# Order of the up projection and place of the state scaling in a fused retention, FFN and routed-FFN kernel

## The chip, the cores and the metric

The kernel runs on one core of one Trainium2 chip. The metric is device time in microseconds (us): the median over the runs of the program. TensorE is called PE here, VectorE DVE, ScalarE ACT and GpSimd POOL, as in the profile.

## The reference, cut to what matters

```python
# 4 batches, 8 heads, 576 positions, 64 per head
ret = (q @ k.T / 8) * gamma_h ** (i - j)        # for i >= j, else 0
x = (ret @ v), heads side by side               # 2304 tokens x 512
h = x @ w_in                                    # 512 x 2048
g = h * tanh(softplus(h))
y = g @ w_out                                   # 2048 x 512
...                                             # routing: 8 experts, 288 tokens each, then relu FFN per expert
```

The change lies in the first two parts: the retention (called attention in the kernel) and the dense FFN. The routing and the expert FFN follow them and are not edited.

## The kernel before, in words

`first_part` computes attention and dense FFN together. The FFN is cut into 9 blocks of 256 tokens times 16 slices of 128 hidden units, which makes 144 **steps** (`plan`, the list `steps`). The first 48 steps mix blocks 0 to 2; from there the blocks follow one another. Each engine executes its instructions in the order in which the Python code issues them, so the loop `for i in range(len(steps) + YL)` is the schedule. In the words of this text, step i issues:

- **S(i)**, the slot work (`slots.get(i)`): for one attention chunk of 128 or 64 positions, in different steps, the scores (`a_scores`, PE L219, DVE L224, POOL L228 and L233), the output (`a_out`, PE L243 and L248, then the evacuation to `xh` on ACT L254 and to `xl` on DVE L255) and the state (`a_state`, PE L273, then the scaling into `SD`, L281 or L285). Transposes and products of the router's logits (`turned`, `products`, L382 to L394) are slot work too.
- **tanh(i)** and the two ACT instructions behind it (`ff_a1`, L327 to L329, tile `d`), then DVE's product and reciprocal (L335, L340), two products on POOL (L347, L348) or one on DVE in steps that convert (L345), and the product with h (`ff_b2`, L353, issued one step later).
- **H(i+1)**, the up projection of the next step (`ff_h`, L318): 12 products of 128x256 into one half of a PSUM tile `ph`. Steps 2m and 2m+1 share a tile; there are two tiles, `ph0` and `ph1`.
- **gh(i-2), gl(i-2)** (`ff_b3`, L359 on ACT, L360 on POOL, or on DVE in steps that convert): the high and low part of g.
- **Y(i-3)**, the down projection (`ff_y`, L412, 6 products of 128x512; in the last block `ff_y_last`, L448, 12 of 128x256). YL is 3.

H(0) is issued ahead of the loop's first step. An H for an odd step may not write its half before tanh of the even step has read the other half of the same tile.

In the steps that still convert the 64-bit weights to float32 halves (`now` or `old` is set; ACT L156, L159, L174, DVE L163, L168, POOL L177), ACT and DVE carry those instructions as well.

The state of a chunk is kept in one PSUM bank as four 128x128 squares of which only two 64x64 blocks on the diagonal are used; the other two blocks hold zeros. `a_state` copies the two blocks into `SD`, times a factor per partition: for chunks 2 to 7 with 8 ACT instructions of 64x64 (L285), for the others with 2 DVE instructions of 64x256 (L281). `a_out` of the next chunk reads `SD` as its weights (L243).

Near the end of the loop `idle` holds short pieces that are issued one or two a step, among them `Grid.pieces` (L637 to L661): DVE takes the largest and smallest logit (L638 to L640, tile `g_mm`), PE transposes them (L644), DVE reduces (L645, L646), PE spreads the result (L650).

Of the kernel before, what the change touches and what calls it, by code (L numbers as in the profile page):

```python
# [15 lines left out]
AF = mybir.ActivationFunctionType  # L16
ALU = mybir.AluOpType

P = 128
# [45 lines left out]
def plan():  # L65


    spread = lambda a, b, n: [a + (b - a) * k // (n - 1) for k in range(n)]
    own = {i: (0, f) for f, i in enumerate([0, 1, 2, 3] + spread(6, ENDS[0], NF - 4))}
    free = [i for i in range(3 * NF) if i not in own]  # L70
    lead = [i for i in free if i < BEGIN2]
    rest = [i for i in free if BEGIN2 <= i]
    near = [i for i in rest if i <= ENDS[1]]
    ones = lead + [near[k] for k in spread(1, len(near) - 1, NF - len(lead))]
    own.update({i: (1, f) for f, i in enumerate(ones)})
    own.update({i: (2, f) for f, i in enumerate(i for i in free if i not in ones)})
    steps = [own[i] for i in range(3 * NF)]
    steps += [(n, f) for n in range(3, NB) for f in range(NF)]
    return steps


def first_part(ctx, tc, att, att_ht, att_hn, dtab, qtab, ktab, stab, wi, wo, wgb, ydram, L, constants, cst, begin, grid):
    nc = tc.nc
# [12 lines left out]
    S_ = big.tile([P, 8, 4], F32, name="st")  # L96
    SD = big.tile([P, 4, P], F32, name="sd")

    steps = plan()
# [42 lines left out]
    class convert:  # L142
# [18 lines left out]
        def x(self):  # L161
            w0 = self.w0
            nc.vector.scalar_tensor_tensor(w0, self.w1, 0x80000000, w0, op0=ALU.bitwise_and,  # L163
                                           op1=ALU.bitwise_or)
# [16 lines left out]
    def x_block(n):  # L181
        if n not in xT:
            if n == 2:
                xT[n] = [sp.tile([P, KT, TB], F32R, tag="x2", name=f"x{k}2", bufs=2) for k in "hl"]
            else:
                xT[n] = [work.tile([P, KT, TB], F32R, tag="x" + k, name="x" + k, bufs=2) for k in "hl"]
        return xT[n]
# [8 lines left out]
    def bank(tag=None):  # L196
        if not tag:
            tag = att_tags[turn[0] % len(att_tags)]
            turn[0] += 1
        return psum.tile([P, 4, P], F32, tag=tag, name="b_" + tag)  # L200
# [3 lines left out]
    def since(ci):  # L204


        b, s0, n = CHUNKS[ci]
        r = CHUNKS[RESTART]
        return s0 - r[1] if ci >= RESTART and b == r[0] else s0
# [47 lines left out]
    def a_state(ci):  # L257
        b, s0, n = CHUNKS[ci]
        if s0 + n == S:
            return  # L260
        a = at_tiles[ci]
        ps_state = state[0]
        if ci == RESTART:
            att_tags.remove("B")
            ps_state = state[0] = bank("B")
            for hp in range(4):
                nc.tensor.matmul(ps_state[:, hp, :], cst["ident"], SD[:, hp, :], start=(hp == 0),
                                 stop=False, skip_group_check=True)
        for hp in range(4):
            for s in range(2):  # L270
                r = slice(s * 64, (s + 1) * 64)
                c = slice((2 * hp + s) * D, (2 * hp + s + 1) * D)
                nc.tensor.matmul(ps_state[r, hp, r], a[:n, 2, c], a[:n, 3, c],  # L273
                                 start=(s0 == 0 and hp == 0), stop=False, skip_group_check=True)
        s0 = since(ci)
        c = (s0 + n + 64) // P - 1 + 4 if (s0 + n) % P else (s0 + n) // P - 1
        for s in range(2):
            r = slice(s * 64, (s + 1) * 64)
            q = slice(s * 64, (s + 1) * 64)
            if ci < 2 or ci > 7:  # L280
                nc.vector.tensor_mul(SD[r, :, q], ps_state[r, :, q],  # L281
                                     S_[r, c, :, None].to_broadcast([64, 4, 64]))
                continue
            for hp in range(4):
                nc.scalar.activation(SD[r, hp, q], ps_state[r, hp, q], AF.Copy, scale=S_[r, c, hp:hp + 1])  # L285

    def chunks_of(n):
        return [ci for ci, (b, s0, l) in enumerate(CHUNKS) if (b * S + s0) // TB == n]
# [13 lines left out]
        return out  # L302

    rs = work.tile([P, DM], BF, tag="scr", name="rs").bitcast(F32)
    q2 = {}
    inv = {}
    hbank = [None]
# [2 lines left out]
    def ff_h(n, f, i):  # L310
        xh, xl = x_block(n)
        if i % 2 == 0:
            hbank[0] = psum.tile([P, 2, TB], F32, tag=("ph0", "ph1")[i // 2 % 2], name="ph")
        ph = hbank[0][:, i % 2, :]
        k = 0
        for kt in range(KT):
            for w, x in ((winh, xh), (winl, xh), (winh, xl)):
                nc.tensor.matmul(ph, w[f][:, kt, :], x[:, kt, :], start=(k == 0), stop=(k == 11))  # L318
                k += 1
        q2[n, f] = ph  # L320

    def ff_a1(n, f, i, alone):

        ph = q2[n, f]
        d = work.tile([P, 2, P], F32, tag="d", name="d", bufs=2)
        df = d.rearrange("p a b -> p (a b)")
        nc.scalar.activation(df, ph, AF.Tanh, scale=0.5)  # L327
        nc.scalar.activation(df, df, AF.Square, bias=half_b, scale=-0.5)  # L328
        nc.scalar.activation(df, df, AF.Copy, bias=0.5, scale=0.5)  # L329
        u = work.tile([P, 2, P], F32, tag="u", name="u", bufs=3)  # L330
        r = u[:, 0, :]
        if alone:

            r = rs[:, i % 2 * P:][:, :P]
        nc.vector.tensor_mul(r, d[:, 0, :], d[:, 1, :])  # L335
        inv[n, f] = (d, u, r, alone)

    def ff_a2(n, f):
        r = inv[n, f][2]
        nc.vector.reciprocal(r, r)  # L340

    def ff_b1(n, f, eng):
        d, u, r, alone = inv.pop((n, f))
        if alone:
            eng.tensor_mul(u, d[:, ::-1, :], r[:, None, :].to_broadcast([P, 2, P]))  # L345
        else:
            eng.tensor_mul(u[:, 1, :], d[:, 0, :], r)  # L347
            eng.tensor_mul(u[:, 0, :], d[:, 1, :], r)  # L348
        gt[n, f] = u.rearrange("p a b -> p (a b)")
# [164 lines left out]
    old, now, nxt = c2, c3, convert()  # L514
# [8 lines left out]
    for n in range(4, NB):  # L523
        ms = micro(n)
        for j, m in enumerate(ms):
            first = 5 if n == 4 else 1
            at = FOUR[j] if n == 4 else int(first + (14 - first) / len(ms) * j)
            slots.setdefault((n - 1) * NF + at, []).extend(m)

    for x in slots.get(-1, []):  # L530
        x()
    for i in range(len(steps) + YL):
        new = i < len(steps)
        if not i:
            ff_h(*steps[0], 0)
        if i == 20:
            constants()
        if i == 62:
            stage.__exit__(None, None, None)
            late = tc.tile_pool(name="late", bufs=1)  # L540
            WG = late.__enter__().tile([P, E, DM], F32, name="WG")
            nc.sync.dma_start(WG, wgb)
        if now:
            now.x()
            now.a()
        if old:
            old.l()
        if new:
            n, f = steps[i]
            for x in slots.get(i, []):  # L550
                x()
            if i and steps[i - 1] in inv:
                ff_b1(*steps[i - 1], nc.vector)
            ff_a1(n, f, i, bool(now or old))
            if i + 1 < len(steps):
                ff_h(*steps[i + 1], i + 1)
        if new:

            eng = nc.vector if now or old else nc.gpsimd
            if i > 1:  # L560
                ff_b3(*steps[i - 2], eng)
            ff_a2(n, f)
            if i:
                ff_b2(*steps[i - 1])
            if eng is not nc.vector:
                ff_b1(n, f, nc.vector if i == len(steps) - 1 else eng)
        if i == len(steps) - 1:
            ff_b2(n, f)
            ff_b3(*steps[i - 1], nc.gpsimd)
            ff_b3(n, f, nc.vector)  # L570
        if now:
            now.h()
        old, now = now, None
        if nxt and i in CONV:
            now, nxt = nxt, convert() if done[0] < len(parts) else None
            now.x1()
            now.c()
        for k in range(2 if i % 4 == 0 or TAIL <= i < POP2 else 1):
            if idle:
                idle.pop(0)()  # L580
        if late and i > TAIL + BEGIN and not idle:
            late = late.__exit__(None, None, None)
            soon.extend(begin())
        if i >= YL:
            ff_y(*steps[i - YL], i)
# [886 lines left out]
def constants(cp, tc, ap, cst):  # L1472
    nc = tc.nc
    load_constants(cp, tc, ap, cst, (("ident", [P, P], F32), ("J", [P, NJ + 1], F32), ("SCL", [P, 3], F32),
                                     ("pri", [P, E], F32), ("tri", [P, P], BF), ("io", [P, 96], BF),
                                     ("pcv", [P, NT, 2], BF), ("WGN", [P, KT, E], F32)))
    cst["ones"] = cp.tile([P, P], BF, name="c_ones")
    nc.vector.memset(cst["ones"], 1.0)
# [69 lines left out]
```

## Time and profile before

| | |
|---|---|
| median of 3 runs | 843.76 us (842.48 to 844.92) |
| the profiled execution | 842.58 us |
| its span, first to last instruction | 840.7 us |
| mean granted PE clock | 0.97 of full speed |
| PE busy | 771.4 us (92%) |
| DVE busy | 541.6 us (64%) |
| POOL busy | 477.9 us (57%) |
| ACT busy | 441.1 us (52%) |
| first H, last Y of the loop | 18.4 us, 541.6 us |

The profile belongs to one execution; all stretches and durations are of it. The 1.9 us between its span and its time lie around the program. The loop takes 523 of the 841 us; behind it come routing and the experts.

### The profile page before, as it was taken

How to read it: one execution, taken by the hardware profiler on the slowest of the kernel's cores; microseconds unless marked ns; L12 is line 12 of the kernel's file. 1: busy time of each engine (PE TensorE's matmuls, PEld its weight loads, DVE VectorE, ACT ScalarE, POOL GpSimd, SP SyncE). 2: the span in 40 equal slices, each digit the busy share in tenths (PEclk: the TensorE clock that was granted, in tenths of full speed). 3: DMA queues.
4: the chain of work that ended last, by engine and by line, in shares of the span. 5: the costliest groups of instructions: out<-in, count | busy, mean ns of one | idle time of the engine just before them, and what ended most of it. 6: DMA issues, size and time to landing. Idle time of an engine off the chain costs nothing.

```text
span 840.7 us, 16293 instructions
## 1 busy us (share of the span) xinstructions
PE 771.4 (92%) x6151; PEld 700.1 (83%) x6151; DVE 541.6 (64%) x1271; ACT 441.1 (52%) x963; POOL 477.9 (57%) x541
## 2 busy tenths in 40 slices
PE   6688999999999999999999999939999999999993
PEld 5677777888888887888888889929989999999993
DVE  4797999555645797887988976576566653442110
ACT  2678999544544554545555554423444543554520
POOL 2543333554445576666766655314777986977811
PEclk9799999999999999999999999958999999999997
DMA  8545442001312310310110000044565664655411
GB/s 315 190 136 202 152 159 101 27 1 51 101 51 101 107 44 2 101 51 27 51 51 26 1 27 2 8 164 143 168 183 180 190 195 155 187 163 170 125 30 32
DMA packets 27321, 87.63 MB, mean 104 GB/s; under 512 B 4449, under 2 KB 5601, under 8 KB 27105
## 3 DMA queue, kind: packets, MB, share of 16 engines
q1 hardware_dynamic: 24160, 77.06, 28.2%
q0 software_dynamic: 3072, 9.44, 3.5%
q8 instruction: 50, 0.82, 0.4%
q14 instruction: 39, 0.31, 0.1%
HBM read 77.05 MB, written 9.44 MB: 103 GB/s over the span
## 4 chain that ended last, share of the span: by engine, by line
PE 64%; DVE 18%; issue 7%; ACT 5%; POOL 2%; DMA 2%; SPq 0%; DVEq 0%; POOLq 0%; ACTq 0%
PE ph L318 18%; PE hp L1263 9%; PE op L1277 8%; PE b_F L412 6%; PE b_E L412 6%; DVE u L340 2%; DVE rs L340 2%; PE cnt L978 2%; DVE raw L163 2%; DVE y L168 1%; DVE u L353 1%; PE b_D L248 1%; DVE u L335 1%; PE b_A L219 1%; PE b_E L448 1%
## 5 line engine op out<-in xcount | busy, mean ns | idle before, releaser
L318 PE MATMUL ph<-xh,winh 128*128 128x256 f32 x576 | 170.5, 296 | 29.0 <-ACT d L327 21.4
L318 PE MATMUL ph<-xl,winh 128*128 128x256 f32 x576 | 161.6, 281 | 1.6 <-DVE xl L255 1.6
L318 PE MATMUL ph<-xh,winl 128*128 128x256 f32 x576 | 161.3, 280 | 0.0
L817 POOL TENSOR_TENSOR wxl<-wraw,wxh 128x1024 fp32r<-128x1024 f32 x60 | 142.3, 2397 | 29.9 <-ACT wxh L815 29.5
L318 PEld LDWEIGHTS ph<-xh,winh 128*128 128x128 f32 x576 | 109.1, 189 | 49.6 <-ACT d L327 28.0
L360 POOL TENSOR_TENSOR gl<-u,gh 128x256 fp32r<-128x256 f32 x114 | 88.6, 778 | 88.0 <-ACT gh L359 87.4
L318 PEld LDWEIGHTS ph<-xh,winl 128*128 128x128 f32 x576 | 109.7, 191 | 2.0
L318 PEld LDWEIGHTS ph<-xl,winh 128*128 128x128 f32 x576 | 109.4, 190 | 2.1 <-DVE xl L255 2.1
L340 DVE RECIPROCAL u<-u 128x128 f32<-128x128 f32 x113 | 107.7, 953 | 3.9
L327 ACT ACTIVATE d<-ph 128x256 f32<-128x256 f32 x144 | 54.5, 379 | 98.1 <-PE ph L318 84.2
L347 POOL TENSOR_TENSOR u<-d,u 128x128 f32<-128x128 f32 x112 | 52.4, 468 | 58.8 <-DVE u L340 58.7
L335 DVE TENSOR_TENSOR u<-d 128x128 f32<-128x128 f32 x113 | 48.3, 427 | 46.4 <-ACT d L329 42.8
L815 ACT ACTIVATE wxh<-wraw 128x1024 fp32r<-128x1024 f32 x64 | 67.3, 1052 | 17.1 <-DMA wraw<-in_wx_dram 17.0
L328 ACT ACTIVATE d<-d,half_b 128x256 f32<-128x256 f32 x144 | 73.5, 511 | 4.7
L348 POOL TENSOR_TENSOR u<-d,u 128x128 f32<-128x128 f32 x112 | 68.2, 609 | 8.8
L359 ACT ACTIVATE gh<-u 128x256 fp32r<-128x256 f32 x144 | 58.5, 406 | 11.3 <-DVE u L353 9.3
L329 ACT ACTIVATE d<-d 128x256 f32<-128x256 f32 x144 | 60.2, 418 | 4.5
L369 DVE SCALAR_TENSOR_TENSOR scr<-y,WG 128x512 bf16<-128x512 f32 x64 | 55.2, 862 | 0.4
L1254 DVE SCALAR_TENSOR_TENSOR htl<-hp,hth 128x288 fp32r<-128x288 f32 x64 | 28.4, 454 | 40.3 <-ACT hth L1266 39.8
L1266 ACT ACTIVATE hth<-hp 128x288 fp32r<-128x288 f32 x64 | 26.1, 408 | 52.3 <-PE hp L1263 51.8
L353 DVE SCALAR_TENSOR_TENSOR u<-u,ph 128x256 f32<-128x256 f32 x144 | 52.5, 365 | 0.3
L1263 PE MATMUL hp<-xth,wxh 128*128 128x288 f32 x256 | 50.2, 309 | 0.9 <-DVE htl L1254 0.9
(271 smaller groups left out, 1885.6 us busy)
## 6 DMA issues: line engine op xcount, KB each, us to landing
wraw<-in_wx_dram SPq DMA_DIRECT2D x64, 512.0 KB, 4.4
att<-in_att_dram SPq DMA_DIRECT2D x32, 512.0 KB, 5.0
raw<-in_wi_dram SPq DMA_DIRECT2D x16, 512.0 KB, 3.3
raw<-in_wo_dram SPq DMA_DIRECT2D x16, 512.0 KB, 3.3
ydram<-y SPq DMA_DIRECT2D x9, 512.0 KB, 2.8
WG<-in_wgb_dram SPq DMA_DIRECT2D x1, 2048.0 KB, 7.6
att<-in_att_ht_dram SPq DMA_DIRECT2D x4, 256.0 KB, 3.8
att<-in_att_hn_dram SPq DMA_DIRECT2D x4, 256.0 KB, 4.1
```

The costliest lines, as they stand in the source:

```text
L318: nc.tensor.matmul(ph, w[f][:, kt, :], x[:, kt, :], start=(k == 0), stop=(k == 11))
L328: nc.scalar.activation(df, df, AF.Square, bias=half_b, scale=-0.5)
L329: nc.scalar.activation(df, df, AF.Copy, bias=0.5, scale=0.5)
L340: nc.vector.reciprocal(r, r)
L348: eng.tensor_mul(u[:, 0, :], d[:, 1, :], r)
L353: nc.vector.scalar_tensor_tensor(g, g, -1.0, q2.pop((n, f)), op0=ALU.add, op1=ALU.mult)
L360: eng.tensor_sub(gl, g, gh.bitcast(F32))
L412: nc.tensor.matmul(py[n][t], g[:, t * P:(t + 1) * P], w[f], start=(f == 0 and w is woh and g is gh), stop=(f == NF - 1 and g is gl))
L815: nc.scalar.activation(hi, raw, AF.Copy)
L817: rest = lambda eng: eng.tensor_sub(lo, raw, hi.bitcast(F32))
L1263: nc.tensor.matmul(hp, W[kt][w][:, s], x[:, kt, :], start=(k == 0), stop=(k == 11))
L1277: nc.tensor.matmul(op, W[4 + ft // 2][w][:, s], h[:, ft, :], start=(k == 0), stop=(k == 23))
```

## The change

The state is scaled with instructions over all 128 partitions and both halves at once: one DVE instruction of 128x512 instead of two of 64x256, or four ACT instructions of 128x128 instead of eight of 64x64. The ACT instructions are no longer issued with the slot work but put into a list, `behind`, and issued behind the three ACT instructions of `ff_a1` of the same step. And H(i+1) is issued in step i only where step i converts weights; in the other steps H(i) is issued at the head of its own step, ahead of S(i).

```diff
@@ a_state
-        for s in range(2):
-            r = slice(s * 64, (s + 1) * 64)
-            q = slice(s * 64, (s + 1) * 64)
-            if ci < 2 or ci > 7:
-                nc.vector.tensor_mul(SD[r, :, q], ps_state[r, :, q],
-                                     S_[r, c, :, None].to_broadcast([64, 4, 64]))
-                continue
+        if ci < 2 or ci > 7:
+            nc.vector.tensor_mul(SD, ps_state, S_[:, c, :, None].to_broadcast([P, 4, P]))
+            return
+
+        def scale():
             for hp in range(4):
-                nc.scalar.activation(SD[r, hp, q], ps_state[r, hp, q], AF.Copy, scale=S_[r, c, hp:hp + 1])
+                nc.scalar.activation(SD[:, hp, :], ps_state[:, hp, :], AF.Copy, scale=S_[:, c, hp:hp + 1])
+
+        behind.append(scale)
@@ first_part
+    behind = []
@@ the loop
+    not_yet = lambda i: steps[i] not in q2
     for i in range(len(steps) + YL):
         new = i < len(steps)
-        if not i:
-            ff_h(*steps[0], 0)
+        if not i or new and not_yet(i):
+            ff_h(*steps[i], i)
...
             ff_a1(n, f, i, bool(now or old))
-            if i + 1 < len(steps):
+            while behind:
+                behind.pop()()
+            if now or old:
                 ff_h(*steps[i + 1], i + 1)
```

Three places show how the instructions stand.

PE, around the output of chunk 7 (step 40; `winh_89` belongs to H(40), `winh_87` to H(41), `woh_116` to Y(36), `woh_117` to Y(37)). Before:

```order
L318 MATMUL ph<-xl,winh_89 128x256
L412 MATMUL b_E<-woh_116,gh 128x512
L412 MATMUL b_E<-wol_132,gh 128x512
L412 MATMUL b_F<-woh_116,gh 128x512
L412 MATMUL b_F<-wol_132,gh 128x512
L412 MATMUL b_E<-woh_116,gl 128x512
L412 MATMUL b_F<-woh_116,gl 128x512
L243 MATMUL b_B<-att,sd 128x128 x4
L248 MATMUL b_B<-pm,att 64x128 x8
L318 MATMUL ph<-xh_602,winh_87 128x256
L318 MATMUL ph<-xh_602,winl_103 128x256
```

The same place now, where lines from L305 on have moved by one:

```order
L319 MATMUL ph<-xl,winh_89 128x256
L243 MATMUL b_B<-att,sd 128x128 x4
L248 MATMUL b_B<-pm,att 64x128 x8
L413 MATMUL b_E<-woh_117,gh 128x512
L413 MATMUL b_E<-wol_133,gh 128x512
L413 MATMUL b_F<-woh_117,gh 128x512
L413 MATMUL b_F<-wol_133,gh 128x512
L413 MATMUL b_E<-woh_117,gl 128x512
L413 MATMUL b_F<-woh_117,gl 128x512
L319 MATMUL ph<-xh_592,winh_87 128x256
L319 MATMUL ph<-xh_592,winl_103 128x256
```

Between H(40) and H(41) stood Y(36) and then S(40); now S(40) comes first and Y(37) behind it.

ACT, around the state of chunk 6 (step 9; `winh_82` and `woh_113` are converted weights). Before:

```order
L254 ACTIVATE xh_602<-b_E 128x4x128
L285 ACTIVATE sd<-b_F,st 64x64 x8
L327 ACTIVATE d<-ph 128x256
L328 ACTIVATE d<-d,half_b 128x256
L329 ACTIVATE d<-d 128x256
L359 ACTIVATE gh<-u 128x256
L174 ACTIVATE woh_113<-y_153 128x512
```

Now:

```order
L254 ACTIVATE xh_592<-b_E 128x4x128
L328 ACTIVATE d<-ph 128x256
L329 ACTIVATE d<-d,half_b 128x256
L330 ACTIVATE d<-d 128x256
L283 ACTIVATE sd<-b_F,st 128x128 x4
L360 ACTIVATE gh<-u 128x256
L174 ACTIVATE woh_113<-y_153 128x512
```

The scaling has moved behind the three instructions of tile `d`, and has half as many instructions.

PE, in step 132 of the last block, around the first transposition of `Grid` (`winh_81` belongs to H(133), `winh_80` to H(132), `woh_109` to Y(129)). Before:

```order
L318 MATMUL ph<-xh,winh_81 128x256
L318 MATMUL ph<-xh,winl_97 128x256
L318 MATMUL ph<-xl,winh_81 128x256
L644 MATMUL b_D<-c_ident,g_mm 2x128
L448 MATMUL b_E<-gh,woh_109 128x256
L448 MATMUL b_E<-gh,wol_125 128x256
```

Now:

```order
L319 MATMUL ph<-xh,winh_80 128x256
L319 MATMUL ph<-xh,winl_96 128x256
L319 MATMUL ph<-xl,winh_80 128x256
L383 MATMUL b_C<-c_ident,y 128x128 x4
L648 MATMUL b_D<-c_ident,g_mm 2x128
L449 MATMUL b_E<-gh,woh_109 128x256
```

H(133) stood between the slot work of step 132 (L382) and the transposition; now the transposition follows the slot work at once.

## Rows read from the trace of the kernel before

**Rows 1.** Stretches: busy us (xcount) of PE, PEld, DVE, ACT, POOL; PEclk, DMA share, GB/s
```profile
90.00:120.00 30.00, 27.07 (x163) 22.00 (x162) 29.16 (x64) 28.25 (x63) 10.32 (x8) 1.00 0.44 147
450.00:480.00 30.00, 29.54 (x220) 25.91 (x219) 28.17 (x57) 16.30 (x39) 20.80 (x31) 1.00 0.00 1
```

**Rows 2.** Waits of PE, 150 to 540 us: us in total, times, longest
```profile
PE ph L318 <- ACT d L327: 7.3, 8, 1.0
PE ph L318 <- DVE u L353: 2.8, 7, 0.5
PE b_A L382 <- ACT y L421: 0.5, 1, 0.5
```

**Rows 3.** Timeline of PE from 177.57 us: start, duration, instruction, idle before
```profile
177.57 1.09 PE L248 MATMUL b_B<-pm,att 128*64 128x128 f32 x16
179.63 0.39 PE L318 MATMUL ph<-xh,winh 128*128 128x256 f32 x1 [0.97 <-ACT d L327]
...
181.11 0.39 PE L412 MATMUL b_E<-woh,gh 128*128 128x512 f32 x1
...
182.48 0.28 PE L318 MATMUL ph<-xh,winh 128*128 128x256 f32 x1
```

**Rows 4.** Timeline of ACT, same stretch
```profile
178.71 0.60 ACT L254 ACTIVATE xh<-b_B 128x512 fp32r<-128x512 f32 x1 [4.49 <-PE b_B L248]
179.20 0.38 ACT L327 ACTIVATE d<-ph 128x256 f32<-128x256 f32 x1
```

**Rows 5.** Waits of DVE, 20 to 150 us
```profile
DVE rs L335 <- ACT d L329: 5.0, 4, 2.1
```

**Rows 6.** Instructions that write tile d, one row: ns min/median/max, first to last start
```profile
L335 DVE TENSOR_TENSOR rs<-d x31: 273/285/1055, 29.2 to 146.0; 128x128 f32<-128x128 f32 x31
```

**Rows 7.** Timeline of ACT, step 9
```profile
73.53 1.82 ACT L285 ACTIVATE sd<-b_F,st 64x64 f32<-64x64 f32 x8
75.37 0.39 ACT L327 ACTIVATE d<-ph 128x256 f32<-128x256 f32 x1
```

**Rows 8.** Timeline of DVE, step 9
```profile
76.78 0.29 DVE L335 TENSOR_TENSOR rs<-d 128x128 f32<-128x128 f32 x1 [2.09 <-ACT d L329]
```

**Rows 9.** Instructions that write tile sd
```profile
L285 ACT ACTIVATE sd<-b_F,st x32: 295/302/309, 32.7 to 75.0; 64x64 f32<-64x64 f32 x32
...
L281 DVE TENSOR_TENSOR sd<-b_B,st x18: 408/422/428, 214.9 to 455.9; 64x256 f32<-64x256 f32 x18
```

**Rows 10.** Instructions that write tile pm
```profile
L224 DVE TENSOR_TENSOR pm<-b_A,dt x15: 409/691/692, 6.5 to 461.2; 128x512 f32<-128x512 f32 x13, 64x256 f32<-64x256 f32 x2
```

**Rows 11.** Timeline of POOL at five places
```profile
173.26 0.73 POOL L360 TENSOR_TENSOR gl<-u,gh 128x256 fp32r<-128x256 f32 x1
...
298.19 1.29 POOL L228 TENSOR_TENSOR att<-att,qt 128x512 f32<-128x512 f32 x1
...
300.50 0.73 POOL L360 TENSOR_TENSOR gl<-u,gh 128x256 fp32r<-128x256 f32 x1
...
470.74 0.74 POOL L360 TENSOR_TENSOR gl<-u,gh 128x256 fp32r<-128x256 f32 x1 [2.83 <-ACT gh L359]
...
537.95 0.74 POOL L360 TENSOR_TENSOR gl<-u,gh 128x256 fp32r<-128x256 f32 x1 [1.13 <-ACT gh L359]
```

**Rows 12.** Timeline of PE: the first product with gl of Y(36), Y(69), Y(119)
```profile
176.12 0.39 PE L412 MATMUL b_E<-woh,gl 128*128 128x512 f32 x1
...
302.60 0.39 PE L412 MATMUL b_E<-woh,gl 128*128 128x512 f32 x1
...
473.53 0.39 PE L412 MATMUL b_E<-woh,gl 128*128 128x512 f32 x1
```

**Rows 13.** Timeline of DVE, end of the first piece of Grid
```profile
502.37 0.16 DVE L640 TENSOR_SCALAR g_mm<-g_mm 128x1 f32<-128x1 f32 x1
```

**Rows 14.** Timeline of PE: the transposition in step 132; first product with gl of Y(142)
```profile
502.74 0.27 PE L644 MATMUL b_D<-c_ident,g_mm 128*2 128x128 f32 x1
...
538.75 0.38 PE L448 MATMUL b_E<-gl,woh 128*128 128x256 f32 x1
```

## The prediction

> **What bounds the kernel now.** I read the busy time by stretch first. From 90 us, while weights are converted, DVE is busy 29.16 of 30 us and PE only 27.07; late in the loop PE is busy 29.54 of 30 and DVE 28.17, at a granted clock of 1.00 in both [rows 1]. So the loop has two parts. In the first one DVE sets the pace, with ACT close behind it; it ends at 146 us, where the tile `rs`, which only steps that convert write, is written for the 31st and last time, so these are steps 0 to 30 [rows 6]. In the second one PE sets the pace, and what can be gained there is what PE waits. The waits of PE from 150 to 540 us sum to 10.6 us in 390, in three lines: 7.3 us in 8 waits of H for tanh, 2.8 us in 7 waits of H for DVE's product with h, and one wait of 0.5 us of a transposition for the evacuated y [rows 2].
>
> One of the 8 is shown. The output of chunk 7 ends on PE at 178.66, and H(41) starts only at 179.63 [rows 3]. In between ACT evacuates that output (0.60 us) and then does tanh(40), which ends at 179.58 [rows 4]. H(41) shares its PSUM tile with H(40), so it must wait for tanh(40); tanh(40) stands behind the evacuation on ACT, and the evacuation waits for S(40). PE has nothing between S(40) and H(41). That is the place that the new order changes.
>
> **The second part: H in its own step.** Before, PE's order was H(i), Y(i-4), S(i), H(i+1). Now it is H(i), S(i), Y(i-3), H(i+1). Number and kind of PE's instructions stay the same. A Y takes 1.37 us (181.11 to 182.48) and an H 1.48 with its late second product [rows 3]. After S(40) PE now has a Y to do, 1.37 us, while tanh(40) comes 0.97 us after S(40): the wait goes, with 0.40 us to spare. The 8 waits are at most 1.0 us each [rows 2], so all of them fit under a Y: **-7.3 us**. The transposition that waited 0.5 us for the evacuated y now stands behind an H: **-0.5**. For the 2.8 us for DVE nothing changes, since H of an even step needs the same product with h as before and as much PE work lies between: 0.
>
> What pays for it is the distance between g and Y. Y(k) stood behind H(k+4), now it stands behind H(k+3): each Y comes a Y and an H earlier against the H of its own g, 1.37 + 1.38 = 2.75 us where H runs without the late product. I set the end of gl(k) and gh(k) against the product of Y(k) that needs it, for k from 32 to 127. In 15 of these 96 Ys there is less than 2.75 us, by 13.0 us in all. Three show it: Y(36), gl ends at 173.99 and its product starts at 176.12, so 2.13 us to spare and 0.6 us missing; Y(69), 301.23 and 302.60, 1.37 to spare and 1.4 missing; Y(119), 471.48 and 473.53, 2.05 and 0.7 [rows 11, 12]. But in all 15 gl or gh was late because it stands behind slot work of step k+2, on POOL (gl(69) behind the products of the scores that begin at 298.19 [rows 11]) or on ACT, and S(k+2) itself now comes a Y earlier, 1.37 us. With that the worst two come out at 0.0 and the others at +0.4 to +0.9. I take **0** here, with a bound of +13.0.
>
> Two places near the end do cost. Grid's transposition starts at 502.74, directly behind H(133), and what it needs from DVE ends at 502.53 [rows 13, 14]. H(133) no longer stands ahead of it; PE comes there 1.4 us earlier with only 0.2 us to spare: **+1.2** (bounds 0 to 1.4, since DVE's piece moves a little earlier too). And at the very end PE already waits for gl: POOL's last gl ends at 538.69 and its product in Y(142) starts at 538.75 [rows 11, 14]. What gl(142) waits for hangs on H(143), the last H, because DVE does the reciprocal of step 143 first. H(143) now has one more Y ahead of it, so this chain moves back by a Y, and nothing is left to fill the gap: **+1.4** (bounds 0.5 to 1.4; a Y of 12 products of the H's shape is taken as long as an H or a Y in [rows 3]).
>
> **The first part: the scaling behind tile d.** H is a step ahead there as before. In steps 1, 3, 7 and 9 ACT scaled the state of a chunk ahead of tanh. In step 9 the 8 instructions took 1.82 us and tanh started at 75.37, at once behind them [rows 7]; DVE had idled 2.09 us when it could begin with the result [rows 8]. These four waits are 5.0 us of a DVE that is otherwise full, the longest 2.1 [rows 5]. Now tanh comes 1.82 us earlier and the scaling stands behind d. It still stands ahead of gh and of the conversion's instructions on ACT, on which DVE waits next. A 64-column instruction takes 0.302 us [rows 9], eight together 1.82, so 0.23 each; one of 256 columns takes 0.38 [rows 4]. Four of 128 columns lie between 0.9 and 1.5 us; I take 1.1, near the 64-column row. So ACT saves 0.7 us per chunk and DVE's own chain 1.8. For steps 1 and 9, where DVE idled 2.1 each, I take 1.1 each, nearer to ACT's gain; the other two waits, 0.8 together, go. **-3.0 us** (bounds -0.6, ACT's least saving twice, and -5.0, the whole of the waits). As DVE is full to the end of this part, this shifts all that follows.
>
> The Trainium skill (ScalarE: Activation LUTs, Rules for kernel authors) budgets some 0.3 us per ACTIVATE and 0.83 ns per element. By it 8 instructions of 64 columns would take 2.8 us and 4 of 128 1.6, a saving of 1.2 us instead of 0.7, an estimate; the sum would be 1.0 us lower with it. The row of one instruction, 0.302 us, is nearly that figure, but eight in 1.82 us overlap, so here the rows decide.
>
> On DVE one instruction of 128x512 takes the place of two of 64x256: 0.69 for 2 x 0.42 us [rows 9, 10]. It saves 0.15 us of DVE per chunk; the products that read `SD` come steps later. I cost it at 0; if DVE's lag were the bound there, nine times 0.15, 1.4 us, would be gained.
>
> **Sum.** -7.3 - 0.5 + 1.2 + 1.4 - 3.0 = -8.2 us. Against the profiled execution, 842.58, that is 834.4; against the median, 843.76, which is 1.2 higher, 835.6. I forecast **835.0 us**, between the two.
>
> **The rivals.** Slower: *Y waits for g*. If the slot work does not bring gl and gh forward (because POOL or ACT reach it no earlier, or because S itself, directly behind H, then waits for DVE to free a bank), all 13.0 us come as new waits of PE before L413: 842.6 - 8.2 + 13.0 = 847.4. It decides from 8.2 of 13.0 on, that is when more than six tenths of the shortage stays. For it: the two worst places have nothing to spare even with the credit. Against it: POOL begins on the scores' operand only when the scores are done, so it does come earlier.
>
> *Given back in part*: a third of the 13.0 stays, 4.3 us: 838.7, or 839.9 from the median. For it: in stretches where DVE is busy 28.17 of 30 us [rows 1] a late row of DVE makes gh and gl late too, and no slot work moves to make up for that.
>
> *No change*: the second part's gain is handed over to DVE, so that the 7.3 us come back as waits for DVE's product, the 2.8 us growing to some 10; what is left is -3.0 + 2.6 - 0.5, so 842. Against it: where DVE is fullest, PE leaves at most 0.5 of 30 us [rows 1], so the 8 waits lie elsewhere, where DVE has more room.
>
> *More*: the first part gives its whole 5.0 us and the two places at the end cost their least, 0.5 together: 842.58 - 7.3 - 0.5 - 5.0 + 0.5 = 830.3.
>
> **How the numbers follow.** Chances: the forecast (832 to 838.5) 0.62; more than that 0.08; given back in part 0.12; no change 0.08; slower 0.10. A measurement of this kernel can tell about 0.3%, 2.5 us, from no change, so faster means below 841.3. The first three cases are faster: 0.82. The fourth is the same, 0.07 of its 0.08; the 0.01 left of it goes to slower, which is 0.11 with the last. The range has the first three cases: 830.3 to 841.0, some 0.8.
>
> **What would show it.** In the profile after: no waits of H for tanh of 1 us between 150 and 360 us; PE's timeline there with L243, L248, then L413, then L319 without a gap. In the first part no DVE wait of 2 us for d in steps 1 and 9, the tile `rs` written for the last time some 3 us earlier, at 143 us. A new wait of about 1.2 us before the transposition L648, and 1.5 us before the product with gl of Y(142). L283's four instructions together near 1.1 us. The forecast is wrong if PE's waits have new lines for L413 with gl or gh as releaser (slower or given back), if its waits for DVE's product grow, or if the last `rs` is not earlier.

## The result, and the profile after

The changed kernel takes 833.46 us (median of 4 runs, 830.91 to 836.3), the kernel before 843.12 in the runs beside it (4 runs, 840.72 to 844.92): a ratio of 0.9888, 95% interval 0.9846 to 0.993. The forecast was 835.0 (830.3 to 841.0). The profiled execution took 832.66 us, span 830.9, granted clock 0.97. The total is as forecast; two terms of the sum behind it are not, and they cancel almost.

The engines' busy time in the page after the change:

```profile
PE 770.4 (93%) x6151; PEld 704.0 (85%) x6151; DVE 537.8 (65%) x1260; ACT 434.4 (52%) x943; POOL 476.9 (57%) x541
```

PE does the same work (770.4 against 771.4 us) in a shorter span. **Second part.** Busy time by stretch, in the columns of [rows 1]; first the sums over 150 to 480 us in eleven stretches of 30, before:

```profile
sum 330.00, PE 320.38 PEld 280.23 DVE 238.81 ACT 166.92 POOL 196.47; mean PE 29.13 PEld 25.48 DVE 21.71 ACT 15.17 POOL 17.86
```

and after, with the last stretch, to be read against the last one of [rows 1]:

```profile
450.00:480.00 30.00, 30.00 (x214) 26.84 (x212) 26.80 (x55) 15.97 (x39) 20.06 (x30) 1.00 0.00 1
sum 330.00, PE 330.00 PEld 295.27 DVE 239.26 ACT 168.43 POOL 202.03; mean PE 30.00 PEld 26.84 DVE 21.75 ACT 15.31 POOL 18.37
```

PE is now busy in all of the 330 us, where 9.6 were lost. The waits of PE from 150 to 540 us, against [rows 2] (the lines L982 and L992 belong to the routing, which now begins before 540):

```profile
PE cnt L982 <- DVE ind L697: 1.2, 1, 1.2
PE b_D L648 <- DVE g_mm L644: 1.0, 1, 1.0
PE b_E L449 <- POOL gl L361: 0.5, 2, 0.3
PE b_E L449 <- ACT gh L360: 0.4, 1, 0.4
PE dg L992 <- DVE full L986: 0.3, 1, 0.3
PE cnt L982 <- ACT y L471: 0.2, 1, 0.2
```

All three lines of [rows 2] are gone, the 2.8 us for DVE among them, and no line of L413 has come. What came is the transposition's wait, 1.0 us, and 0.9 us of waits for gl and gh in the last block.

**First part.** Here nothing was gained. The waits of DVE from 20 to 150 us, against [rows 5]:

```profile
DVE raw L163 <- ACT raw L159: 3.5, 3, 1.8
DVE gl L361 <- ACT gh L360: 1.0, 1, 1.0
DVE pm L224 <- PE b_D L219: 0.4, 1, 0.4
```

The 5.0 us for `d` are gone, as forecast. But the row of `rs` that answers to [rows 6], and DVE's row of `gl`, are

```profile
L336 DVE TENSOR_TENSOR rs<-d x31: 276/285/1380, 28.9 to 147.0; 128x128 f32<-128x128 f32 x31
...
L361 DVE TENSOR_TENSOR gl<-u,gh x30: 412/420/1518, 41.2 to 530.4; 128x256 fp32r<-128x256 f32 x30
```

The last `rs` is at 147.0, not at 143 and not even at 146.0; and a product for `gl` that has a median of 0.42 us took up to 1.52. Before, its longest took 0.43. DVE works longer on about as many instructions (busy time by stretch, 30 to 90 us, before, then after; the third column is DVE's):

```profile
30.00:60.00 30.00, 24.44 (x250) 21.65 (x250) 26.56 (x49) 22.66 (x59) 13.10 (x10) 0.91 0.38 116
60.00:90.00 30.00, 25.92 (x198) 22.23 (x197) 25.43 (x52) 26.44 (x66) 11.50 (x9) 0.94 0.60 209
```

```profile
30.00:60.00 30.00, 24.45 (x250) 21.19 (x249) 28.31 (x46) 21.35 (x50) 12.53 (x9) 0.93 0.35 112
60.00:90.00 30.00, 24.39 (x190) 19.79 (x189) 28.23 (x53) 24.28 (x56) 11.65 (x9) 1.00 0.62 201
```

From the first `rs` to the last DVE issues 217 instructions in both kernels. Its idle time there fell from 6.6 to 2.0 us (new waits among them, 1.0 us of `gl` for gh), but the durations of the 217 sum to 127.7 us instead of 121.6. The largest part of these 6.1 us is that of `gl` (DVE's products from 20 us to the last `rs`: count, sum of us and mean ns, before, then after):

```profile
L360 DVE TENSOR_TENSOR gl<-u,gh 128x256 fp32r<-128x256 f32 x28 | 11.7, 418 | 0.0
...
L361 DVE TENSOR_TENSOR gl<-u,gh 128x256 fp32r<-128x256 f32 x28 | 15.0, 536 | 1.0 <-ACT gh L360 1.0
```

What lies beside a long one, in step 5 (timeline of DVE, then of POOL, after the change):

```profile
56.55 0.28 DVE L336 TENSOR_TENSOR rs<-d 128x128 f32<-128x128 f32 x1
56.75 1.50 DVE L361 TENSOR_TENSOR gl<-u,gh 128x256 fp32r<-128x256 f32 x1
58.18 0.94 DVE L341 RECIPROCAL rs<-rs 128x128 f32<-128x128 f32 x1
...
56.62 1.36 POOL L177 TENSOR_TENSOR wol<-y,woh 128x512 fp32r<-128x512 f32 x1 [2.66 <-ACT woh L174]
```

POOL's subtraction of the conversion began 0.13 us ahead of the product and ended at 57.98; the product ended at 58.25. In the same step of the kernel before, the product began 0.11 us ahead of the subtraction and kept its 0.41 us; the subtraction took 1.46 us, where its median is 1.29:

```profile
56.53 0.41 DVE L360 TENSOR_TENSOR gl<-u,gh 128x256 fp32r<-128x256 f32 x1
56.87 0.93 DVE L340 RECIPROCAL rs<-rs 128x128 f32<-128x128 f32 x1
...
56.64 1.46 POOL L177 TENSOR_TENSOR wol<-y,woh 128x512 fp32r<-128x512 f32 x1 [2.11 <-ACT woh L174]
```

### The profile page after: what moved, and what is told of

It is laid out like the page before. It is cut to its first block, busy times and chain, and to the rows that moved or that the text cites. A ratio compares the mean times of both kernels' runs of the same rounds, so it can differ in the third digit from the quotient of the medians.

```text
span 830.9 us, 16266 instructions
## 1 busy us (share of the span) xinstructions
PE 770.4 (93%) x6151; PEld 704.0 (85%) x6151; DVE 537.8 (65%) x1260; ACT 434.4 (52%) x943; POOL 476.9 (57%) x541
## 4 chain that ended last, share of the span: by engine, by line
PE 72%; DVE 13%; issue 7%; ACT 3%; POOL 2%; DMA 2%; SPq 0%; DVEq 0%; POOLq 0%; ACTq 0%
PE ph L319 20%; PE hp L1267 9%; PE b_E L413 8%; PE op L1281 8%; PE b_F L413 8%; DVE rs L341 2%; DVE raw L163 2%; PE cnt L982 2%; DVE y L168 2%; PE b_A L219 2%; PE b_D L248 1%; DVE u L346 1%; DVE hot L878 1%; PE b_E L449 1%; PE b_F L449 1%
## 5 line engine op out<-in xcount | busy, mean ns | idle before, releaser
L319 PE MATMUL ph<-xh,winh 128*128 128x256 f32 x576 | 165.1, 287 | 19.1 <-ACT d L328 12.0
L361 POOL TENSOR_TENSOR gl<-u,gh 128x256 fp32r<-128x256 f32 x114 | 85.7, 752 | 95.5 <-ACT gh L360 94.7
L336 DVE TENSOR_TENSOR u<-d 128x128 f32<-128x128 f32 x113 | 40.3, 357 | 69.7 <-ACT d L330 68.0
```

Source lines behind the costliest of these rows:

```text
L361: eng.tensor_sub(gl, g, gh.bitcast(F32))
```

## The experiments

**Theory.** All of the gain comes from the order of H. In the first part the waits for `d` did go, but DVE's instructions that take two operands from SBUF are held while POOL's subtraction L177 runs, and with an earlier tanh they meet it. **Rivals.** The scaling has a part in the second part's gain; or the scaling behind `d` delays gh and the conversion on ACT, so that DVE waits there.

All runs but 3 and 4 in one table. "Last rs" is the end of the range in the row of `rs`; "loop" is the last start of the product `b_F<-gl,woh` less that; "behind" is the span less that start. All three are of the profiled execution; times and ratios are of all runs. The kernel before was run again beside each group, with a median of 843.95 us beside runs 1 and 2, 841.98 beside 5 to 8 and 843.49 beside 9 to 12, so across groups the ratios compare, not the times.

| kernel | last rs | loop | behind | median us | ratio to before (95%) |
|---|---|---|---|---|---|
| before | 146.0 | 395.3 | 299.4 | 843.12 | |
| changed | 147.0 | 385.7 | 298.2 | 833.46 | 0.9888 (0.9846 to 0.993) |
| 1 scaling alone | 146.8 | 394.9 | 300.2 | 843.65 | 1.0002 (0.9988 to 1.0017) |
| 2 order of H alone | 146.4 | 385.6 | 300.5 | 833.89 | 0.9877 (0.9853 to 0.9902) |
| 5 reciprocal first | 156.8 | 385.2 | 298.7 | 842.63 | 1.0002 (0.9989 to 1.0016) |
| 6 subtraction in halves | 148.5 | 385.0 | 298.3 | 833.59 | 0.9899 (0.9874 to 0.9924) |
| 7 Y ahead of S | 148.2 | 414.7 | 298.1 | 862.21 | 1.0235 (1.0216 to 1.0255) |
| 8 grid behind Y | 147.1 | 384.2 | 299.1 | 831.68 | 0.9872 (0.9852 to 0.9891) |
| 9 four ahead of tanh | 146.5 | 385.6 | 300.0 | 835.23 | 0.99 (0.9879 to 0.9921) |
| 10 later L174 | 145.5 | 385.8 | 301.0 | 834.65 | 0.9889 (0.9868 to 0.991) |
| 11 old scaling, grid | 148.6 | 384.5 | 300.6 | 832.66 | 0.9868 (0.9847 to 0.9889) |
| 12 later L174, grid | 145.9 | 384.4 | 300.5 | 832.31 | 0.986 (0.9837 to 0.9882) |

The loop repeats within some tenths of a us wherever its code is the same (385.0 to 385.8 in six kernels). The part behind it, which no kernel edits, spreads over 2.9 us, so totals say nothing on 1 or 2 us.

**1. The scaling alone.** The changed scaling, every H at its old place:

```diff
-        if not i or new and not_yet(i):
-            ff_h(*steps[i], i)
+        if not i:
+            ff_h(*steps[0], 0)
...
-            if now or old:
+            if i + 1 < len(steps):
                 ff_h(*steps[i + 1], i + 1)
```

> The changed scaling (one instruction on DVE, four on ACT behind tile d) with the old place of every H. Theory (the second part's gain comes from the order of H alone, and the first part's gain is eaten by DVE instructions that get longer beside POOL's conversion subtraction): the 8 waits of PE for tanh are back, 7 to 8 us between 150 and 540 us; tile rs written for the last time at 146.5 to 147.5 us; total 842 to 845 us, no gain over the kernel before. Rival (DVE's nine shorter scalings make room for PE's waits to go): at least 3 us of the 10.6 us of waits are gone and the total is 841 or less.

Measured: ratio 1.0002, loop 394.9. The waits of PE from 150 to 540 us are back:

```profile
PE ph L319 <- ACT d L328: 7.3, 8, 1.0
PE ph L319 <- DVE u L354: 2.2, 5, 0.5
PE b_A L383 <- ACT y L422: 0.5, 1, 0.5
```

The scaling brings nothing by itself; DVE's nine shorter instructions take 0.6 us at most off the waits for DVE.

**2. The order of H alone.** The changed loop, with the old `a_state`, in place and in halves:

```diff
-        if ci < 2 or ci > 7:
-            nc.vector.tensor_mul(SD, ps_state, S_[:, c, :, None].to_broadcast([P, 4, P]))
-            return
...
+        for s in range(2):
+            r = slice(s * 64, (s + 1) * 64)
+            q = slice(s * 64, (s + 1) * 64)
...
-        behind.append(scale)
```

> The new place of H with the old scaling in place (eight instructions of 64x64 on ACT ahead of tanh, two of 64x256 on DVE). Theory: all of the gain is here; PE waits between 150 and 480 us stay under 1.5 us, tile rs is written for the last time at 145.5 to 146.5 us as before, and the total is 0 to 1.5 us below the changed kernel, 831 to 834 us. Rival (the scaling carries a part of the second part's gain, since nine chunks save 0.15 us of DVE each and four have 0.7 us of ACT less): waits of PE of 1 to 3 us remain between 150 and 480 us, and the total is 834 to 837 us.

Measured: ratio 0.9877, loop 385.6, as the changed kernel within 0.1. From 150 to 480 us no wait of H or Y is left; L648 waits 0.9. The whole gain is the order of H.

**3 and 4. Without the subtraction.** In both kernels `lo` is set to zero once, by POOL, and L177 is left out, so the low parts of the weights are missing. That changes the logits and with them the routing, and the part behind the loop grows to some 700 us; only the first part is compared.

```diff
         def l(self):
-            nc.gpsimd.tensor_sub(self.lo, self.t, self.hi.bitcast(F32))
+            pass
```

> The kernel before without POOL's subtraction in the conversion (L177): the low parts of the weights are left out (set to zero once), so POOL has none of these instructions of 1.28 us. Theory (DVE instructions with two operands in SBUF get longer while that subtraction runs): DVE's product for gl never takes over 0.6 us in steps 1 to 30, and tile rs is written for the last time 1 to 4 us earlier than 146.0 us. Rival (their length has nothing to do with POOL): single products for gl of 1.5 us stay.

> The changed kernel with the same left out as in the run before it. Theory (the 5.0 us of waits did go, and longer DVE instructions beside POOL's subtraction ate them): no product for gl over 0.6 us, and tile rs is written for the last time 2 to 5 us earlier than in the kernel before with the same left out. Rival (the scaling behind d delays gh and the conversion's instructions on ACT, so DVE waits there instead): it is written within 1 us of that kernel or later.

Measured, the rows of `rs`, before without it and changed without it:

```profile
L337 DVE TENSOR_TENSOR rs<-d x31: 275/287/898, 28.6 to 144.3; 128x128 f32<-128x128 f32 x31
```

```profile
L338 DVE TENSOR_TENSOR rs<-d x31: 271/285/1128, 27.9 to 141.7; 128x128 f32<-128x128 f32 x31
```

Without the subtraction the changed kernel is 2.6 us earlier, with it 1.0 later. Each is one execution, and with the subtraction the last `rs` of one and the same code came out up to 2.6 us apart (run 11), so the size is not sure. The sums point the same way: without it DVE's durations between the first and the last `rs` differ by 1.0 us (119.3 and 120.3) instead of 6.1, while the idle time still falls, from 8.1 to 5.2. So most of the 3.0 us of the forecast was there to be had. One product for `gl` still took 1.25 us, against the expectation; it lay beside another POOL product that reads SBUF (49.15, 1.42 us, `att<-att,kt`).

**5. The reciprocal first.** In the converting steps DVE does the reciprocal, then the product for `gl`:

```diff
+            first = eng is nc.vector
+            if first:
+                ff_a2(n, f)
             if i > 1:
                 ff_b3(*steps[i - 2], eng)
-            ff_a2(n, f)
+            if not first:
+                ff_a2(n, f)
```

> The changed kernel; in the steps that convert, DVE's reciprocal of the step is issued ahead of its product for gl (and ACT's gh behind it in program order, which leaves ACT's own order alone). Theory (the product for gl gets longer while POOL's subtraction L177 runs, the reciprocal does not): the reciprocal of 0.95 us now lies beside the subtraction of 1.28 us, no product for gl is over 0.8 us, the last write of tile rs falls to 142.5 to 145.5 us, the total to 828.5 to 831.5. Rival (a late gl holds up something else in these steps, or DVE's time was not lost there): last rs at 146 us or later, total at 832 or more.

Measured: the opposite, last `rs` at 156.8 and 842.63 us. The row of `gl` and two places (DVE, then POOL):

```profile
L361 DVE TENSOR_TENSOR gl<-u,gh x30: 360/860/967, 42.4 to 539.7; 128x256 fp32r<-128x256 f32 x30
...
103.43 0.29 DVE L336 TENSOR_TENSOR rs<-d 128x128 f32<-128x128 f32 x1
103.76 0.95 DVE L341 RECIPROCAL rs<-rs 128x128 f32<-128x128 f32 x1
104.63 0.86 DVE L361 TENSOR_TENSOR gl<-u,gh 128x256 fp32r<-128x256 f32 x1
...
103.93 1.27 POOL L177 TENSOR_TENSOR winl<-y,winh 128x512 fp32r<-128x512 f32 x1 [2.76 <-ACT winh L174]
```

The reciprocal is not held, as the theory says. But I had looked at the three bad steps only. The subtraction outlasts the reciprocal, so now the product is held until 0.27 to 0.29 us behind the subtraction's end (here 105.20 and 105.49) in 25 of the row's 30. In the changed kernel most steps have the product start just ahead of the subtraction:

```profile
102.14 0.42 DVE L361 TENSOR_TENSOR gl<-u,gh 128x256 fp32r<-128x256 f32 x1
102.48 0.95 DVE L341 RECIPROCAL rs<-rs 128x128 f32<-128x128 f32 x1
...
102.44 1.30 POOL L177 TENSOR_TENSOR winl<-y,winh 128x512 fp32r<-128x512 f32 x1 [2.12 <-ACT winh L174]
```

The 28 products for `gl` up to the last `rs` sum to 21.8 us instead of 15.0: 6.8 of the 9.8 us that the last `rs` came later. In the rows above the reciprocal starts 0.33 us behind the start of the product that it reads, where the product for `gl` started 0.20 behind it; over 28 steps that is some 3.6 us, an estimate, and the other rows gave a little back. The same DVE work in another order costs 9.8 us of time.

**6. The subtraction in halves.**

```diff
-            nc.gpsimd.tensor_sub(self.lo, self.t, self.hi.bitcast(F32))
+            hi = self.hi.bitcast(F32)
+            for q in (slice(0, 256), slice(256, 512)):
+                nc.gpsimd.tensor_sub(self.lo[:, q], self.t[:, q], hi[:, q])
```

> The changed kernel with POOL's subtraction L177 as two instructions of 128x256. If DVE's product is held until the running POOL instruction ends, and then goes on between two of them: the three products for gl that took 1.5 us take 0.8 to 1.1, and the last write of tile rs is 0.7 to 2 us earlier than 147.0 us, total 831 to 833. If both share the memory all through: the three stay at 1.3 to 1.6 us, and the last rs at 146.5 to 147.5, total 832 to 835.

Measured: no product for `gl` over 0.97 us, but the last `rs` at 148.5. Step 5 again (DVE, POOL):

```profile
56.40 0.86 DVE L348 TENSOR_TENSOR u<-d,rs 128x256 f32<-128x256 f32 x1
57.19 0.81 DVE L338 TENSOR_TENSOR rs<-d 128x128 f32<-128x128 f32 x1
57.93 0.41 DVE L363 TENSOR_TENSOR gl<-u,gh 128x256 fp32r<-128x256 f32 x1
...
56.23 1.62 POOL L179 TENSOR_TENSOR wol<-y,woh 128x256 fp32r<-128x256 f32 x2 [2.38 <-ACT woh L174]
```

Each of two DVE instructions is held for one half (0.81 us each) and then runs; that is holding by the instruction, not sharing all through, which would have left the `gl` at 1.3 to 1.6. It gains nothing: two shorter holds take the place of a long one.

**7. Y ahead of S.** In steps that don't convert, Y(i-3) goes behind H(i) and S(i) behind it.

```diff
+            if ahead:
+                ff_y(*steps[i - YL], i)
             for x in slots.get(i, []):
...
-        if i >= YL:
+        if i >= YL and not ahead:
```

(`ahead` is set where `new and i >= YL and not (now or old)`.)

> The changed kernel with Y(i-3) ahead of S(i), directly behind H(i), in the steps that don't convert. Theory (a Y between S and the next H covers ACT's evacuation and tanh, and the slot work that comes a Y earlier is what brings gl and gh in time): the 7 to 8 us of waits of H for tanh come back, and the Ys wait for gl or gh by 3 to 13 us in sum, total 843 to 853. Rival (the Ys were never short, the 13.0 us of the forecast's bound were an error of its own): only the waits for tanh come back, Ys wait under 2 us, total 839 to 842.

Measured: 862.21, the worst kernel of all and above both expectations. The waits of PE from 150 to 560 us:

```profile
PE ph L319 <- ACT d L328: 10.2, 12, 1.0
PE b_E L413 <- ACT gh L360: 5.8, 9, 0.9
PE b_E L413 <- POOL gl L361: 5.0, 7, 0.7
PE b_E L449 <- ACT gh L360: 1.2, 2, 0.8
PE b_E L449 <- POOL gl L361: 0.8, 3, 0.3
PE b_C L413 <- POOL gl L361: 0.7, 1, 0.7
PE b_C L413 <- ACT gh L360: 0.6, 1, 0.6
```

Without S between Y and the next H the waits for tanh return and grow to 10.2, and 12.1 us of waits of L413 for gl and gh come, close to the 13.0 us of shortage that the forecast had before it credited S. Against the changed kernel S and Y change places (and the pieces of `idle` come behind Y), so S ahead of Y does both: the Y behind it covers tanh, and gl and gh come in time. How much of the latter is S coming earlier and how much Y coming later is not told apart. These waits are 24.3 us, 22.4 more than in the changed kernel; the loop grew by 29.0, and the other 6.6 are not assigned to rows.

**8. The grid behind Y.** In the last steps the pieces of `idle` come behind `ff_y`.

```diff
+        if i >= YL and i >= TAIL:
+            ff_y(*steps[i - YL], i)
         for k in range(2 if i % 4 == 0 or TAIL <= i < POP2 else 1):
             if idle:
                 idle.pop(0)()
...
-        if i >= YL:
+        if i >= YL and i < TAIL:
             ff_y(*steps[i - YL], i)
```

> The changed kernel with the pieces of the grid issued behind the Y of the same step in the last steps, so that a Y lies between H(133) and the transposition L648. Theory (the wait of 1.0 us is there only because nothing covers it): the wait is gone, total 1.0 us lower, 831.5 to 833. Rival (the wait moves to the next piece of the chain, or DVE's pieces come later by as much): a wait of PE of 0.5 us or more in this place stays, total as the changed kernel.

Measured: the line `b_D L648` is gone from the waits, and the loop is 1.5 us shorter (384.2): as the theory says. In runs 11 and 12 the same edit gives 384.5 and 384.4. The waits in the routing behind it did not grow. The total, 831.68, lies where the theory had it, but the ratio's interval overlaps the changed kernel's, so the total alone shows no gain.

**9. Four instructions ahead of tanh.**

```diff
-        behind.append(scale)
+        scale()
```

> The changed kernel with ACT's four scaling instructions at the old place, with the slot work ahead of tanh; DVE's one instruction and the order of H as in the changed kernel. Theory (with tanh late again, h and so POOL's subtraction come late too, behind the start of DVE's product for gl): DVE waits for d again, 3 to 5 us in steps 1 to 9, no product for gl over 1.0 us, last write of tile rs at 145 to 146.5 us, total 831.5 to 834. Rival (the collisions come from the shorter scaling itself, not from its place): products for gl of 1.5 us stay and the last rs is at 147 us or later.

Measured: last `rs` at 146.5, 835.23 us, waits for `d` of 1.4 us only, and the three products for `gl` of 1.5 us still there, in the same steps 4 to 6. The theory as I put it here falls: the place behind `d` is not needed for the meeting.

**10. A later L174.** In converting steps with slot work ACT issues L174, on which L177 waits, behind L159.

```diff
-        if now:
+        wait = bool(slots.get(i)) and now and nxt and i in CONV
+        if now and not wait:
             now.h()
...
             now.x1()
+            if wait:
+                old.h()
```

> The changed kernel; in the converting steps that also have slot work, ACT's conversion instruction L174, on which POOL's subtraction waits, is issued one instruction of 0.66 us later (behind L159). Theory (in those steps DVE reaches its product for gl late, and the subtraction begins just ahead of it): the subtraction now begins behind the product's start, at most one product for gl is over 1.0 us, DVE is busy 2 to 4 us less between the first and the last write of tile rs, the last is at 143.5 to 146 us, and the total 829.5 to 832. Rival (the 0.66 us only moves the overlap to another DVE instruction of the same kind): busy time falls by less than 1 us, last rs 146 to 148, total 832 to 835.

Measured: last `rs` at 145.5, 1.5 us earlier; DVE's instructions between the first and the last `rs` sum to 125.7 us, 2.0 less than in the changed kernel. But three products for `gl` of 1.5 us are there, now in steps 2, 4 and 7, and the total, 834.65, is above what I expected; the ratio is the changed kernel's. In the profiled execution the part behind the loop took 301.0 us, the most of all.

**11 and 12. Two combinations.** The edits of 2 and 8, and of 8 and 10.

> The new place of H and the grid's pieces behind Y, with the old scaling in place (the second run's edit and the eighth's). Theory (the scaling is worth -1 us in the first part as changed, the grid's wait 1.0): 0.5 to 2 us below the changed kernel, 831 to 833. Rival (the two gains are noise of the part behind the loop): 833 or more.

> The changed kernel with the later conversion instruction of the tenth run and the grid's pieces behind Y of the eighth. Theory: the two gains add up, 2 to 4 us below the changed kernel, 828 to 831. Rival (the later conversion instruction gains nothing): 831 to 833, as the eighth run.

Measured: 832.66 and 832.31 us. Their loops are 1.1 and 1.4 us shorter than without the grid's edit (runs 2 and 10). For run 12 the theory's 828 to 831 is missed; the total lies where the rival has it. Run 11 has the code of run 2 in steps 0 to 30, yet its last `rs` is at 148.6 instead of 146.4, with long products for `gl` that run 2 had not:

```profile
L361 DVE TENSOR_TENSOR gl<-u,gh x30: 409/419/1523, 41.0 to 530.8; 128x256 fp32r<-128x256 f32 x30
```

So whether DVE or POOL comes first is decided by some tenths of a us, and differs between executions of the same code. The last `rs` shows it: the old scaling gives 146.0, 146.4 and 148.6, the new one 147.0, 146.8, 148.2 and 147.1. Run 12 has the lowest ratio, but its interval and the changed kernel's overlap; neither combination is shown to be faster than the changed kernel.

## Why the prediction was right in its sum and wrong in two terms

- **"The 8 waits ... -7.3 us", "-0.5".** Right. They are gone, run 1 has them back, run 2 loses them without the scaling. PE is busy in every us of 150 to 480.
- **"For the 2.8 us for DVE nothing changes ... 0".** Wrong: they are gone too. I looked at the work of PE between H and the product with h, which is the same, but not at when DVE gets there. S's work on DVE now comes a Y earlier, as I credited for POOL and ACT in the next paragraph, but not here. One place (steps 75 to 77): DVE's scaling in S(75), then ACT's last instruction for `d` of step 77 and DVE's first product with it, before,

```profile
312.00 0.85 DVE L281 TENSOR_TENSOR sd<-b_B,st 64x256 f32<-64x256 f32 x2
...
316.87 0.42 ACT L329 ACTIVATE d<-d 128x256 f32<-128x256 f32 x1
...
318.66 0.82 DVE L335 TENSOR_TENSOR u<-d 128x128 f32<-128x128 f32 x1
```

  and the same after, with the product of step 76:

```profile
306.42 0.68 DVE L278 TENSOR_TENSOR sd<-b_B,st 128x512 f32<-128x512 f32 x1
...
310.47 0.29 DVE L336 TENSOR_TENSOR u<-d 128x128 f32<-128x128 f32 x1 [1.08 <-ACT d L330]
...
312.71 0.42 ACT L330 ACTIVATE d<-d 128x256 f32<-128x256 f32 x1
...
313.64 0.81 DVE L336 TENSOR_TENSOR u<-d 128x128 f32<-128x128 f32 x1
```

  DVE was 1.37 us late behind `d` and is 0.51 late now. Before, it worked almost without a gap from the scaling to this product; now the scaling comes sooner and DVE even idles 1.08 us before step 76. Over the 113 steps behind the first part DVE was over 1 us late in 36 before and in 7 after. That the earlier S is the cause is argued from such places; no run takes it away alone (run 7 does, but there PE waits so much for tanh, gl and gh that no wait of H for DVE comes).
- **"I take 0 here, with a bound of +13.0."** Right: no L413 waits. That it hangs on S ahead of Y is shown by run 7.
- **"+1.2" for the transposition.** Measured 1.0; run 8 takes it away.
- **"+1.4" at the end.** The two lines of L449 show 0.9, and the stretch from the end of the last H to that of the last Y tells about the same: it has a Y of 1.4 us less to do and fell only from 7.4 to 7.2 us, so some 1.2 were paid.
- **"-3.0 us" in the first part.** The step that failed. The waits did go ([rows 5]), and ACT's four instructions took 1.13 us where I took 1.1, but I set a gain of DVE's time equal to its waits and took the durations of DVE's own instructions as fixed. They depend on what POOL does beside them: DVE idled 4.6 us less and its instructions took 6.1 us more, 3.3 of it in `gl`. Measured: 1.0 us later instead of 3.0 earlier, with nothing to tell that from 0 in the spread of the same code; without the subtraction, 2.6 us earlier (runs 3 and 4). By the forecast's own sign, the last `rs` not earlier, this part was wrong.

In sum the loop behind the first part gave 9.6 us where the forecast had 5.2 (7.3 + 0.5 - 1.2 - 1.4): 2.8 more from the waits for DVE, 0.7 from the two costs (1.0 and 0.9 for 2.6); some 0.9 is not assigned to rows. The first part gave 4.0 less. The span fell by 9.8, of which 1.2 lie behind the loop, where nothing was changed. So the mechanism was right for the waits for tanh and for gl and gh; that the total also came within 2 us of the forecast is luck, since two errors of about 4 us went against each other. The rival "no change" had the gain handed to DVE, which was wrong in the second part, and right in kind in the first.

## What to carry to other kernels

Work that only feeds a later step, but that another engine needs early, belongs ahead of the bound engine's long independent work, so that this work covers the other engine's chain: one such exchange on PE took away all waits of three kinds. When a DVE wait is to be taken away, look at what runs on POOL in the time into which DVE's next instructions move: an instruction with two SBUF operands that starts just behind a POOL instruction can take as long as that one, and what was gained is gone. Before an order is changed for a few steps, look at the steps in which it already works.

## What was not expected of the hardware

A DVE product of two SBUF operands that starts while POOL's subtraction (two SBUF operands too) runs nearly always ends about 0.28 us behind it, however short it is by itself: 0.42 us became 1.50 (58.25 against 57.98), or 0.86 (105.49 against 105.20). In the first parts of all runs with the whole subtraction, 46 of 48 products for `gl` that started while it ran ended 0.27 to 0.29 us behind it. The other two are step 4 of the kernel before and of run 2: before, the product started 0.37 us behind the subtraction's start (51.11) and kept 0.41 us, and the subtraction took 1.92, so there POOL was held. DVE's reciprocal, with one operand, keeps its 0.95 us at the same place. With the subtraction in halves, each hold lasts one half. The Trainium skill (SBUF — State Buffer, SBUF: two separate sides and Who interferes with whom) says that a DVE instruction with two SBUF inputs contends with a GpSimd instruction that reads SBUF, and that the one that starts first has the shared ports for its whole length. The trace agrees in both, by the numbers above (in step 5 before, the product was first and the subtraction took 1.46 us instead of 1.29). By that rule the question for the forecast's first part would have been where L177 starts, and the nearer bound of its -3.0 would have been 0.
